# Projection groups of a segmented memory transformer regrouped: five groups instead of seven, one left unit per segment, and a new order of all items

## The chip, the cores and the metric

The kernel runs on one core of one Trainium2 chip. The time is device microseconds of one execution on that core; the time of a version is the median of its runs. The profile is of one execution.

The engines are named as the profile names them: PE is TensorE (matmuls), PEld its weight loads, DVE VectorE, ACT ScalarE, POOL GpSimd, SP the engine that issues nearly all DMAs here.

## The reference, cut to what matters

The model is 640 wide. Branch A is attention over 64 segments of 32 rows. Every segment puts 8 memory rows in front of its 32 rows, computes Q, K and V for 32 heads of 192, masks, takes the softmax, multiplies by V and projects back with Wo. The first 8 rows of the result are the memory of the next segment, so the segments are a serial chain. Branch B is a gated feed-forward network, and a gate mixes the two.

```
for s in range(n_seg):
    h = concat([mem, x[:, 32*s : 32*s + 32]])
    q, k, v = h @ Wq, h @ Wk, h @ Wv            # 32 heads x 192 = 6144 columns each
    p = softmax(where(mask, q @ k.T * scale, -1e9))
    o = (p @ v) @ Wo
    mem = o[:, :8]
    outs.append(o[:, 8:])
a = concat(outs)
b = (gelu(x @ w_gate) * (x @ w_up)) @ w_down
return g * a + (1 - g) * b                      # g = sigmoid(x . gate_w)
```

## The kernel before, in words

**Start.** The feed-forward branch is computed first and its rows are stored in DRAM. While it runs, weights of the attention are loaded. Then the loop over the 64 segments begins.

**What is "left".** Of a segment's 32 rows of x, the last 8 (the left rows) don't fit beside the 24 others and the 8 memory rows in the 32 rows that one projection handles. Their Q and K don't depend on the memory. They are computed ahead, for four segments at once (a group g of four segments has 4 x 8 = 32 left rows), in left units: one unit is Q and K of one eighth-group of heads, and needs five items `lf` (k = 0..4, two lists of four matmuls each, L899 and the helper L226), then two items `le` that evict and transpose the rows (ACT L904, DVE L906) and store them in DRAM (L910, or L1300 for two halves in mid-segment). Where units are placed is said by LUNIT: for every place (the segment number modulo 4) a map from unit number to head group. Their V (`Vl`) is computed beside V in segments of place 0; one head group's is computed at the end of place 3 (items `vb`, L1034). The output projection of the left rows is done in place 3 beside the ordinary one (`wo_left`).

**Head groups and pieces.** The 32 heads are four groups of 8. For each group, Q, K and V come from five weight pieces (k = 0..4, 128 rows x 1536 columns, 384 KB); the Wo matrix is 16 pieces of 480 KB. Not all fit: the pieces of the first and the last head group share places in SBUF (13 of their 15 projection pieces, and 3 Wo pieces). When the matmul that reads a piece is issued, `swap_loads` (through `load_piece`, L611) puts a load of the partner into SP's queue; odd segments run through the head groups backwards, so every segment loads 16 pieces. For the first group's K the issue is held back until the group's last item, so that Q pieces go first.

**Projection items.** An item ("g", n, k) runs k-step k of projection group n. GROUPS[n] lists which (matrix, head group) pairs it holds: matrix 0 is Q, 1 is K, 2 is V. All lists of a step use the same 32 rows as weights, so the first list loads them (L1061) and the others keep them (`_matmul_kept`, L226). Each list is four matmuls of 384 columns in four column strips of TensorE. After the last step, ACT evicts each result from PSUM, V first where the group has it (L1084 for V, L1081 for Q and K).

**The other items**, in the order of one head group's way: `tq` and `tk` transpose Q and K rows (DVE L1095; POOL L1098 copies part of Q); `sc` puts the mask and the scores in PSUM (L1106, L1114, L234, L1121), and DVE takes maximum and difference (L1133, L1135); `ex` is the rest of the softmax (ACT L1145, DVE L1147, L1149, L1151, L1152); `pt` transposes the probabilities on TensorE (L1168, L1173) and ACT evicts them (L1186); `pv` is the value product (L1201, L1203, evicted by ACT L1212 and, for the last group, also DVE L1217); `wo` is the output projection (L1230 for the first three groups in two items each, L1253 for the last). After the last `wo`, DVE adds (L1395) and transposes (L1399) the new memory into the operand of the next segment.

**What sets the order.** PROG is a list written out by hand, one for all segments; every engine gets its instructions in the order of this list and waits on semaphores. Items of other places are skipped. PSUM banks are handed out by `misc_bank`: the least recently used of banks 0 to 3, bank 4 in places 1 and 2 (in place 3 for groups below 3), bank 7 for groups 0 and 1, leaving out those held by an open left unit. An `le` item behind the last of the other items in PROG is put off until after the segment's end.

## Time and profile before

| | |
|---|---|
| median of 3 runs | 1770.06 us (1767.09 to 1770.34) |
| profiled execution | 1771.21 us |
| its span, first to last instruction | 1769.4 us |
| granted TensorE clock, mean over the span | 0.997 |
| first projection matmul of segment 0 | 178.3 us into the span |
| last matmul of segment 63 | 1763.0 us into the span |
| mean length of a segment in place 0, 1, 2, 3 (segments 4 to 59) | 25.12, 24.94, 23.38, 25.64 us |
| bytes moved by DMA | 499.58 MB, mean 282 GB/s |

The span is what the profile's times refer to; the time of an execution is a little longer. A segment's length is from its first projection matmul to that of the next one.

In the profile a group is a source line with an engine, an operation and a shape; for each it gives busy time, mean length of one instruction, and the idle time of the engine before it with what ended that idle time. Where no semaphore ended it, the profile writes "issue". The lengths of matmuls are modelled and overlap, so the pace of TensorE is read from the starts of successive matmuls.

### The profile page before, as it was taken

The numbers are of one execution on the slowest core, as the hardware profiler recorded it, in microseconds if no ns is written. First come the engines' busy times: TensorE is split into PE (matmuls) and PEld (weight loads), VectorE is DVE, ScalarE is ACT, GpSimd is POOL, SyncE is SP. The second block draws the span as 40 slices with busy tenths as digits, with TensorE's granted clock in tenths as the row PEclk, the third lists the DMA queues.
The fourth block names the chain that finished last, engine by engine and source line by source line (L and its number), as shares of the span: only waits on it lengthen the run. The fifth ranks groups of instructions, "written<-read, shape, count | busy, mean of one in ns | idle before, by whom it ended". The sixth has DMA issues, their size and how long they took to land.

```text
span 1769.4 us, 80660 instructions
## 1 busy us (share of the span) xinstructions
PE 1606.2 (91%) x39162; PEld 798.4 (45%) x31501; DVE 959.9 (54%) x2934; ACT 803.3 (45%) x1835; POOL 400.6 (23%) x1358
## 2 busy tenths in 40 slices
PE   9999899989998999889999998988998899989987
PEld 4554444444444444444444444444444444444443
DVE  2222655556565655556555555555565655655554
ACT  3222544545444544445444544444444454444443
POOL 1100222222222222222222222222222222222222
PEclk9999999999999999999999999999999999999999
DMA  9914987888778887878778886878787887879776
GB/s 319 310 45 153 328 314 258 318 306 292 275 271 310 298 312 254 308 289 313 279 273 293 306 314 226 318 283 300 275 284 288 296 315 259 312 276 326 283 277 236
DMA packets 271313, 499.58 MB, mean 282 GB/s; under 512 B 105304, under 2 KB 132208, under 8 KB 270960
## 3 DMA queue, kind: packets, MB, share of 16 engines
q1 hardware_dynamic: 267832, 491.34, 78.2%
q8 instruction: 276, 4.52, 1.0%
q10 hardware_dynamic: 3128, 3.09, 0.5%
q14 instruction: 77, 0.63, 0.1%
HBM read 473.22 MB, written 21.11 MB: 279 GB/s over the span
## 4 chain that ended last, share of the span: by engine, by line
PE 66%; DVE 17%; issue 6%; DMA 5%; ACT 4%; POOL 1%; DVEq 0%; SPq 0%; ACTq 0%; POOLq 0%
PE ps L1061 18%; PE ps L226 14%; PE ps L1230 8%; DMA arena<-in_A_Wo_dram 4%; PE ps L818 3%; PE ps L1201 3%; PE ps L815 3%; PE ps L899 3%; DVE ps L1135 2%; PE ps L1106 2%; DVE arena L1133 2%; PE ps L833 2%; DVE arena L1147 2%; PE ps L1253 2%; DVE arena L1095 2%
## 5 line engine op out<-in xcount | busy, mean ns | idle before, releaser
L1061 PE MATMUL ps<-arena 128*32 128x384 bf16 x9940 | 727.7, 328 | 52.2 <-DVE arena L1399 33.6
L226 PE MATMUL ps<-arena 128*32 128x384 bf16 x7680 | 595.3, 327 | 7.8 <-DVE arena L1239 3.5
L1061 PEld LDWEIGHTS ps<-arena 128*32 128x32 bf16 x9940 | 259.5, 97 | 377.0 <-issue 238.3
L1095 DVE STREAM_TRANSPOSE arena<-arena 128x384 bf16<-128x384 bf16 x512 | 270.6, 557 | 151.3 <-ACT arena L1081 150.3
L1081 ACT ACTIVATE arena<-ps 128x384 bf16<-128x384 f32 x512 | 236.2, 489 | 213.6 <-PE ps L1061 193.2
L1230 PE MATMUL ps<-arena 128*32 128x320 bf16 x6144 | 294.7, 300 | 15.1 <-issue 12.4
L1145 ACT ACTIVATE ps<-ps 104x160 f32<-104x160 f32 x256 | 71.9, 281 | 285.3 <-DVE ps L1135 285.3
L1230 PEld LDWEIGHTS ps<-arena 128*32 128x32 bf16 x6144 | 163.3, 96 | 76.8 <-issue 19.2
L1133 DVE TENSOR_REDUCE arena<-ps 104x4 f32<-104x160 f32 x256 | 82.9, 324 | 163.0 <-PE ps L1121 163.0
L1212 ACT ACTIVATE arena<-ps 128x480 bf16<-128x480 f32 (+1 forms) x256 | 137.0, 535 | 42.5 <-PE ps L1203 37.8
L1098 POOL COPY arena<-arena 64x160 bf16<-64x160 bf16 x256 | 81.3, 318 | 325.3 <-DVE arena L1095 314.2
L1186 ACT ACTIVATE arena<-ps 128x448 bf16<-128x448 f32 x192 | 104.2, 543 | 99.7 <-PE ps L1173 99.1
L1220 POOL COPY arena<-arena 128x96 bf16<-128x96 bf16 x256 | 68.2, 266 | 356.8 <-ACT arena L1212 267.6
L1084 ACT ACTIVATE arena<-ps 128x384 bf16<-128x384 f32 x256 | 125.1, 489 | 26.4 <-PE ps L1061 21.1
L1147 DVE TENSOR_REDUCE arena<-ps 104x4 f32<-104x160 f32 x256 | 83.0, 324 | 93.4 <-ACT ps L1145 93.4
L1201 PE MATMUL ps<-arena 128*64 128x160 bf16 x1536 | 122.1, 242 | 12.1 <-ACT arena L1186 5.8
L1201 PEld LDWEIGHTS ps<-arena 128*64 128x64 bf16 x1536 | 80.8, 109 | 89.1 <-issue 31.6
L899 PE MATMUL ps<-arena 128*32 128x384 bf16 x1280 | 112.7, 332 | 2.4 <-issue 2.4
L956 POOL COPY arena<-arena 128x96 bf16<-128x96 bf16 x256 | 70.3, 275 | 194.1 <-PE ps L1121 130.2
L1203 PE MATMUL ps<-arena 128*64 128x64 bf16 x1536 | 104.8, 194 | 3.9 <-issue 3.9
L1239 DVE TENSOR_TENSOR arena<-ps,arena 64x160 f32<-64x160 f32 x160 | 50.8, 317 | 75.2 <-ACT arena L1236 60.9
L906 DVE STREAM_TRANSPOSE arena<-arena 128x384 bf16<-128x384 bf16 x128 | 73.7, 576 | 31.7 <-ACT arena L904 27.5
(88 smaller groups left out, 2040.7 us busy)
## 6 DMA issues: line engine op xcount, KB each, us to landing
arena<-in_A_Wk_dram SPq DMA_DIRECT2D x335, 384.0 KB, 7.3
arena<-in_A_Wv_dram SPq DMA_DIRECT2D x335, 384.0 KB, 9.1
arena<-in_A_Wo_dram SPq DMA_DIRECT2D x205, 480.0 KB, 6.4
arena<-in_A_Wq_dram SPq DMA_DIRECT2D x209, 384.0 KB, 5.1
arena<-left_qk_scratch SPq DMA_DIRECT2D x126, 96.0 KB, 3.0
left_qk_scratch<-arena SPq DMA_DIRECT2D x49, 192.0 KB, 2.4
left_qk_scratch<-arena SPq DMA_DIRECT2D x30, 96.0 KB, 5.9
ffn_b_scratch<-arena ACTq DMA_DIRECT2D x16, 160.0 KB, 3.8
```

What stands on the lines that cost most here:

```text
L226: return e.add_instruction(mybir.InstMatmult(name=nm, start_tensor_calc=like["start"], stop_tensor_calc=stop, tile_size=(128, 32), tile_po ...
L899: fns.append(lambda e, outp=outp, rhs=rhs, j=j: e.matmul(outp, lhs, rhs, start=(k == 0), stop=(k == KT - 1), tile_position=(0, 32 * j)))
L1061: fns.append(lambda e, outp=outp, rhs=rhs, j=j: e.matmul(outp, lhs, rhs, start=(k == 0), stop=(k == KT - 1), tile_position=(0, 32 * j)))
L1081: S_.add("act", lambda e, m=m, bk=bk: e.activation(out=rows_sb[m], in_=ps[:, bk, 0:384], func=ACTF.Copy), reads=[r_ps[bk]], writes=[r_rows ...
L1084: S_.add("act", lambda e, i=i, bk=bk: e.activation(out=v_sb[i % NVB].rearrange("p (c n) -> p c n", c=3), in_=ps[:, bk, 0:384].rearrange("p ...
L1095: S_.add("dve", lambda e: e.transpose(out=dst[:, :, 0:L], in_=rows_sb[m].rearrange("p (c r) -> p c r", r=L)), reads=[r_rows[m]], writes=[r ...
L1133: S_.add("dve", lambda e: e.tensor_reduce(out=mxs, in_=S3, axis=AX.X, op=ALU.max), reads=[rb], writes=[rst], name="smax max")
L1147: S_.add("dve", lambda e: e.tensor_reduce(out=sms, in_=S3, axis=AX.X, op=ALU.add), reads=[rb], writes=[rst], name="smax sum")
L1201: return [lambda e: e.matmul(full, v[:, e0:e0 + 64], PTm[:, i], start=True, stop=False, tile_position=(0, 64 * i), skip_group_check=True), ...
L1203: lambda e: e.matmul(part, vl[:, e0:e0 + 64], PTl[:, i], start=False, stop=True, tile_position=(0, 64 * i), skip_group_check=True)]
L1212: S_.add("act", lambda e: e.activation(out=apx(u[:, 0, 0, :], [[R, na], [3 * R, 4], [1, R]]), in_=ps[:, A, 0:na * W].rearrange("p (c t r) ...
L1230: fns.append(lambda e, i=i, t=t, j=j, gv=gv: e.matmul(ps[32 * j:32 * j + 32, bank, 0:2 * DJ].rearrange("p (h n) -> p h n", h=2), lhs2[i], ...
```

## The change

Three things change, all of them data of the schedule; no instruction gets another shape.

1. GROUPS goes from seven groups to five. Q and K of a head group always stand in one group, with the V of the head group before: (Q0, K0), (V0, Q1, K1), (V1, Q2, K2), (V2, Q3, K3), (V3). Before, K2 and K3 were groups of their own and Q2 and Q3 stood with the preceding V.
2. LUNIT has one left unit in every place: head groups 3, 0, 2, 1 in places 0, 1, 2, 3. Before, place 1 had two (1 and 0) and place 3 none. The units that place 3 owes are computed ahead of the loop for the first groups, so five units stand there instead of four.
3. PROG is written anew. The scores of head group 1 stand just ahead of value product 0, the scores of 2 and the P transpose of 1 stand inside the fourth projection group, and value product 1 follows that group. The last Wo item is the last of all items, so every `le` item stands ahead of the segment's end, and none is in mid-segment.

```diff
-    GROUPS = [[(0, 0), (1, 0)], [(2, 0), (0, 1), (1, 1)], [(2, 1), (0, 2)], [(1, 2)], [(2, 2), (0, 3)], [(1, 3)], [(2, 3)]]
+    GROUPS = [[(0, 0), (1, 0)], [(2, 0), (0, 1), (1, 1)], [(2, 1), (0, 2), (1, 2)], [(2, 2), (0, 3), (1, 3)], [(2, 3)]]
...
-    PROG = [("g", 0, 0), ("g", 0, 1), ("g", 0, 2), ("g", 0, 3), ("g", 0, 4), ("tq", 0), ("g", 1, 0), ("tk", 0),
-            ("g", 1, 1), ("g", 1, 2), ("sc", 0), ("g", 1, 3), ("ex", 0), ("g", 1, 4), ("tq", 1), ("g", 2, 0),
-            ("g", 2, 1), ("g", 2, 2), ("lf", 1, 0, 0), ("pt", 0), ("g", 2, 3), ("tk", 1), ("g", 2, 4), ("g", 3, 0),
-            ("sc", 1), ("g", 3, 1), ("lf", 1, 0, 1), ("g", 3, 2), ("ex", 1), ("g", 3, 3), ("g", 3, 4), ("g", 4, 0),
-            ("lf", 1, 0, 2), ("pv", 0), ("lf", 1, 0, 3), ("g", 4, 1), ("tk", 2), ("g", 4, 2), ("pt", 1), ("g", 4, 3),
-            ("tq", 2), ("g", 4, 4), ("sc", 2), ("ex", 2), ("lf", 1, 0, 4), ("pv", 1), ("g", 5, 0), ("le", 1, 0, 0),
-            ("g", 5, 1), ("lf", 0, 1, 0), ("g", 5, 2), ("wo", 0, 0), ("le", 1, 0, 1), ("tq", 3), ("pt", 2), ("g", 5, 3),
-            ("wo", 0, 1), ("g", 5, 4), ("pv", 2), ("tk", 3), ("lf", 0, 1, 1), ("lf", 1, 1, 0), ("wo", 1, 0), ("sc", 3),
-            ("lf", 2, 1, 0), ("wo", 1, 1), ("g", 6, 0), ("lf", 2, 1, 1), ("lf", 1, 1, 1), ("g", 6, 1), ("ex", 3),
-            ("g", 6, 2), ("wo", 2, 0), ("lf", 1, 1, 2), ("pt", 3), ("g", 6, 3), ("lf", 2, 1, 2), ("g", 6, 4),
-            ("wo", 2, 1), ("lf", 2, 1, 3), ("lf", 1, 1, 3), ("pv", 3), ("lf", 0, 1, 2), ("lf", 2, 1, 4), ("lf", 1, 1, 4),
-            ("vb", 0), ("le", 1, 1, 0), ("vb", 1), ("vb", 2), ("vb", 3), ("le", 1, 1, 1), ("le", 2, 1, 0),
-            ("lf", 0, 1, 3), ("lf", 0, 1, 4), ("wo", 3, 0), ("le", 2, 1, 1), ("le", 0, 1, 0), ("wo", 3, 1), ("le", 0, 1, 1),
-            ("vb", 4)]
+    PROG = [("g", 0, 0), ("g", 0, 1), ("g", 0, 2), ("g", 0, 3), ("g", 0, 4), ("g", 1, 0), ("g", 1, 1), ("g", 1, 2),
+            ("tq", 0), ("tk", 0), ("sc", 0), ("g", 1, 3), ("ex", 0), ("g", 1, 4), ("tq", 1), ("g", 2, 0),
+            ("g", 2, 1), ("tk", 1), ("g", 2, 2), ("pt", 0), ("g", 2, 3), ("g", 2, 4), ("sc", 1), ("tq", 2),
+            ("pv", 0), ("g", 3, 0), ("tk", 2), ("g", 3, 1), ("g", 3, 2), ("ex", 1), ("lf", 2, 1, 0), ("sc", 2),
+            ("pt", 1), ("g", 3, 3), ("ex", 2), ("g", 3, 4), ("pv", 1), ("lf", 2, 1, 1), ("lf", 1, 1, 0), ("tk", 3),
+            ("lf", 0, 1, 0), ("tq", 3), ("lf", 2, 1, 2), ("wo", 0, 0), ("lf", 1, 1, 1), ("pt", 2), ("lf", 3, 1, 0),
+            ("wo", 0, 1), ("g", 4, 0), ("pv", 2), ("sc", 3), ("wo", 1, 0), ("wo", 1, 1), ("wo", 2, 0), ("ex", 3),
+            ("g", 4, 1), ("wo", 2, 1), ("lf", 0, 1, 1), ("g", 4, 2), ("pt", 3), ("g", 4, 3), ("g", 4, 4),
+            ("lf", 1, 1, 2), ("lf", 2, 1, 3), ("lf", 3, 1, 1), ("lf", 0, 1, 2), ("lf", 3, 1, 2), ("lf", 3, 1, 3),
+            ("vb", 0), ("lf", 2, 1, 4), ("pv", 3), ("lf", 1, 1, 3), ("lf", 0, 1, 3), ("le", 2, 1, 0),
+            ("lf", 1, 1, 4), ("le", 1, 1, 0), ("vb", 1), ("le", 1, 1, 1), ("vb", 2), ("le", 2, 1, 1),
+            ("lf", 0, 1, 4), ("vb", 3), ("lf", 3, 1, 4), ("vb", 4), ("wo", 3, 0), ("le", 3, 1, 0), ("le", 0, 1, 0),
+            ("le", 0, 1, 1), ("le", 3, 1, 1), ("wo", 3, 1)]
...
-    LUNIT = ({1: 3}, {0: 1, 1: 0}, {1: 2}, {})
+    LUNIT = ({1: 3}, {1: 0}, {1: 2}, {1: 1})
```

## The prediction, as it was put on record

> **What bounds the kernel.** I read the page, then the busy time of four successive segments, then the timelines of all engines inside one of them, then the DMA rows, the waits and the clock. A list below is four matmuls of 384 columns (one weight piece against the 32 rows of a segment); P0 to P3 is the segment number modulo 4; times inside a segment count from its first projection matmul.

> ```profile
> PE 1606.2 (91%) x39162; PEld 798.4 (45%) x31501; DVE 959.9 (54%) x2934; ACT 803.3 (45%) x1835; POOL 400.6 (23%) x1358
> ...
> PE 66%; DVE 17%; issue 6%; DMA 5%; ACT 4%; POOL 1%; DVEq 0%; SPq 0%; ACTq 0%; POOLq 0%
> ```
> TensorE is the bound on average, with a third of the chain elsewhere. The same by segment, P0 to P3 in order:
> ```profile
> 969.70:994.85 25.15, 22.87 (x612) 11.82 (x492) 15.49 (x49) 12.26 (x29) 5.75 (x20) 1.00 0.79 279
> 994.85:1020.74 25.89, 22.51 (x592) 10.89 (x452) 15.21 (x47) 12.47 (x29) 5.05 (x19) 1.00 0.81 284
> 1020.74:1043.60 22.86, 20.93 (x553) 10.00 (x434) 13.79 (x44) 11.55 (x27) 6.43 (x21) 1.00 0.89 318
> 1043.60:1067.88 24.28, 23.00 (x629) 12.54 (x530) 12.54 (x42) 11.03 (x26) 6.67 (x22) 1.00 0.81 296
> ```
> The first column after the window is the length, the next the matmul busy time. Over segments 4 to 59 the mean lengths are 25.12, 24.94, 23.38 and 25.64 us, together 99.08; 64 segments are 1585 of the 1769.4 us.

> Two other things bound a segment. **Weights**: 13 projection pieces and 3 output pieces come in per segment, each into the place of one just used.
> ```profile
> L611 SPq DMA_DIRECT2D arena<-in_A_Wk_dram x5: 333/432/442, 1021.3 to 1025.8; - x5
> ...
> DMA to landing us min/median/max: 4.3/5.7/6.7
> ```
> ```profile
> L611 SPq DMA_DIRECT2D arena<-in_A_Wo_dram x3: 328/430/432, 1034.5 to 1035.3; - x3
> ...
> DMA to landing us min/median/max: 5.1/6.0/6.7
> ```
> The last K piece is issued at 1025.8 and lands 6.7 later, 11.75 us into this P2 segment; the last Wo piece lands at 1042.0, 21.3 in. The pieces queue behind each other (about 1 us each), so their landing hangs on when the first group frees places, not on when they are wanted. Medians over all segments: last K piece at 12.48, 13.83, 12.82, 12.43 (P0 to P3; earliest of P3 11.54), last Wo piece at 21.9, 23.6, 21.7, 21.5.

> **Refill of TensorE's instructions**:
> ```profile
> PEld ps L1061 <- issue: 238.3, 819, 2.6
> ...
> PEld ps L1168 <- DVE arena L1152: 82.1, 148, 1.0
> ```
> ```profile
> 1008.96 0.66 PE L1061 MATMUL ps<-arena 128*32 128x384 bf16 x9 [1.04 <-issue]
> ```
> Numbering all matmuls and weight loads, every stop of this kind falls on the same instruction of 256 (the instruction queue's packets are 16 KB). There are 267 such borders in the loop; 87 cost over 0.25 us, 73 us in all: 0.82, 0.90, 0.68, 2.16 us per segment in P0 to P3. The stop depends on how fast the 256 before it went: over 6 us it is 0.02 on average, 5 to 5.5 us 0.41, 4 to 4.5 us 1.00.

> **Part by part. Weight loads.** Before, 5 of a segment's 12 projection lists per k keep the weights of the list before; after, 7 (groups of 2, 3, 3, 3, 1). That removes 2x5x4 = 40 loads per segment, 2560 in all. I take no gain:
> ```profile
> 1020.92 0.34 PE L226 MATMUL ps<-arena 128*32 128x384 bf16 x4
> 1021.08 0.34 PE L1061 MATMUL ps<-arena 128*32 128x384 bf16 x4
> ...
> 1021.24 0.34 PE L226 MATMUL ps<-arena 128*32 128x384 bf16 x4
> ...
> 1021.40 0.34 PE L1061 MATMUL ps<-arena 128*32 128x384 bf16 x4
> ```
> Lists with own weights (L1061) and kept ones (L226) both start 0.163 us after the one before. The other end is 2560 x 26 ns (259.5 us over 9940 loads) = 67 us gained. [...]

> **Work per segment.** From the timelines: 60 lists x 0.163 = 9.78; four scores at 0.48, four P transposes at 0.10, four value products at 0.52; six Wo items at 0.407; the last two with their entry 0.96; from the last matmul to the next segment's first 0.87 (DVE's sums and transposes). That is 18.45. A left unit is 5 x 0.325 = 1.63; P0 adds 15 left-value lists, 2.45; P3 adds 7 left Wo items at 0.407 and 5 lists, 3.67. Before: 22.5, 21.7, 20.1, 22.1; lengths less work leave stalls of 2.6, 3.25, 3.3, 3.5. After, P1 loses a unit to P3: 22.5, 20.1, 20.1, 23.75. The sum is the same; the start-up gains a unit and the loop loses one.

> **K3 moved forward.** After, Q3 and K3 stand in the fourth group. Ahead of its end are 55 lists (8.95), three scores (1.44), two P transposes (0.2) and one value product (0.52): 11.1 us, 11.4 in P2 with a left item. Its last K list can't start before the last K piece lands, 12.4 to 12.8, and ends 0.16 later. The same pieces were wanted at 14 to 15.6 before, and TensorE's weight loads waited 1.9 us for them in the whole trace. Behind the waiting list stand, on TensorE, all that follows in the segment, and through it the evictions of V2, Q3 and K3 on ACT and everything that these release. P1's 13.83 becomes about 12.7, because the store that delayed its first K load to 1.62 (0.54 elsewhere) is no longer issued behind the segment's end. So TensorE waits 1.7, 1.55, 1.5 us in P1, P2, P3; none to 0.1 in P0, whose left-value lists (10 x 0.163) and bank wait bring it to about 13. This wait covers softmax 1: from score 1's end DVE needs 0.34 + 0.34, two transposes 1.05, then 0.34 + 0.19 + 0.29 + 0.18 = 2.7, over the 2.45 of TensorE work laid beside it.

> **What goes.** The wait for P transposes 2 and 3 (0.9, 0.55, 0.8, 0.4 by place): softmax 2 ends near 13.95, its transpose is wanted at 14.5 to 15, and softmax 3 (2.1 us) has three or four Wo items beside it. P1's lateness of Wo pieces goes too: two mid-segment stores leave SP's queue and the first K piece starts 1.1 earlier, so the last Wo lands near 21.7. With the 1.3 from the last Wo item to the next segment this is a floor of about 23.0.

> **What is late next.** P0 keeps its wait for the bank of the left sums before Q2 (released by DVE L1239, 0.4) and for the copied Q of score 0 (POOL L1098, 0.17; in the others it is in the rest). P0: the left rows are all ahead of the Z sums on DVE now; two transposes (0.49 apart) end 1.6 after the first last-Wo item starts, the sums were due at 1.13: 0.5. Value product 3 waits for V3's eviction (0.49): 0.3 in P0, 0.45 in P1, 0.15 in P2. P2: the bank of value product 1 is V2's, evicted only after the group's last V list: 0.35; nothing stands between value product 3 and the last Wo: 0.55 for its eviction; small ones 0.5 (P transpose 2's eviction 0.15, softmax 3 0.2, Z 0.15). P1: 0.35 of the same small ones, 0.1 for Wo. Moved DMAs: the left stores go out just before the next segment's stage load on SP; P0's first K piece then lands like P2's, 4.7 instead of 4.1, which its work covers.

> **Refill.** 40 instructions fewer of 1072 per segment. Behind the K wait P3 has 640 in 11.3 us (4.5 us per 256), P1 about 480 in 9.4 (5.0): as dense as before. I take 0.85, 0.6, 0.7, 2.1. Ends: half of it, or half more.

> **Sum.** Stalls after: P0 refill 0.85, bank 0.4, Qz 0.17, V3 0.3, tail 0.5, rest 0.25 = 2.45; P1 0.6 + 1.7 + 0.45 + 0.35 + 0.1 + 0.25 = 3.45; P2 0.7 + 1.55 + 0.35 + 0.55 + 0.15 + 0.5 = 3.8; P3 2.1 + 1.5 + 0.3 = 3.9. Lengths: 24.95, 23.55, 23.9, 27.65 = 100.05 against 99.08: +0.97 per four, 16 times +15.5. The profiled execution took 1771.2 (span 1769.4), 1.1 over the median of 1770.06; so 1770.06 + 15 is **1785**, its own range 1767 to 1802.

> **Rivals.**
> A, refill stops halve (0.13): -36, **1749**. For: fewer instructions, and the K wait stretches the blocks that hold it. It decides at 6 us per block of 256, in the half behind the K wait. Against: that half is as dense as before.
> B, on the other side as well (0.11): the K pieces come in time. If the last one lands by 11.0, P3 gets 1.5 back, P2 0.4, P1 0.1: 32 us, **1753**. Against: the earliest of P3 was 11.54.
> C, slower (0.18): the refill stops grow by half, or the clock gate drops in the waits: **1822**.
> ```profile
> 1685.80:1689.20 3.40, 1.79 (x64) 1.22 (x60) 1.67 (x7) 0.97 (x3) 1.14 (x3) 1.00 0.11 28
> 1689.20:1692.60 3.40, 3.32 (x44) 0.91 (x24) 0.71 (x4) 0.14 (x1) 0.72 (x3) 0.50 0.49 135
> ```
> A 3.4 us window with 1.79 busy is followed by one with a granted clock of 0.50; this happens three times in the loop, 1.7 us lost each. One in two of P1 to P3's waits would cost 24 x 1.7 = 41. Against: a K wait of 3.8 us holds 2.5 us of work. [...]
> D, weight loads set the pace after all (0.03): -67, **1718**.

> **Chances.** Forecast 0.55, of it 0.09 within and 0.02 below the 0.2% (3.5 us) that a measurement of this kernel can tell from no change. Faster 0.13 + 0.11 + 0.03 + 0.02 = 0.29, same 0.09, slower 0.44 + 0.18 = 0.62. The range takes in A, B and most of C: 1748 to 1820.

> **What would show it.** Weight loads 28,941 and equal pace of L1061 and L226; waits of L226 or L1061 for in_A_Wk of some 1.5 us in P1 to P3, near zero in P0; no wait left at L1168 for L1152 in the second half; P1 shorter by 1.4, P3 longer by 2. I am wrong if K waits stay under 0.5, if P3 grows by less than 1, or if refill stops leave 50 to 95 us.

## The result, and the profile after

The changed kernel takes 1777.74 us (median of 8 runs, 1774.39 to 1786.39); the kernel before took 1770.44 us beside it (8 runs). The ratio is 1.0046, 95% interval 1.0024 to 1.0068: slower, by 7 us, where 15 were forecast. The profiled execution took 1774.39 us (span 1772.6), the shortest of the eight, so the two traces (1771.21 and 1774.39) show only 3 us of the 7; where the other 4 lie, no trace shows.

Lines of the changed kernel are one lower than those of before from L611 on (L1061 is L1060, L1399 is L1398); helper L226 keeps its number. The page of the changed kernel, the busy line and the two lines of the chain, by engine and by source line:
```profile
PE 1580.3 (89%) x39181; PEld 741.7 (42%) x28941; DVE 945.5 (53%) x2934; ACT 781.4 (44%) x1835; POOL 399.5 (23%) x1358
...
PE 59%; DMA 24%; DVE 8%; ACT 5%; issue 3%; SPq 1%; POOL 0%; DVEq 0%; ACTq 0%; POOLq 0%
DMA arena<-in_A_Wk_dram 20%; PE ps L226 14%; PE ps L1060 12%; PE ps L1229 11%; PE ps L1200 4%; DVE arena L905 3%; PE ps L898 3%; PE ps L814 3%; PE ps L817 3%; DMA arena<-in_A_Wo_dram 3%; PE ps L832 2%; PE ps L1105 2%; ACT arena L1185 1%; DVE arena L1238 1%; ACT arena L903 1%
```
2560 weight loads are gone, as counted. DMA's share of the chain went from 5% to 24%: in 45 of the 64 segments the chain now runs through the landing of a K piece; before, it did in one. The same by segment (28 to 31, P0 to P3; columns as in the prediction):
```profile
875.58:899.14 23.56, 22.11 (x613) 10.65 (x454) 15.75 (x50) 11.94 (x28) 5.74 (x20) 1.00 0.88 306
899.14:922.35 23.21, 20.20 (x553) 8.94 (x393) 13.43 (x44) 11.28 (x27) 5.74 (x20) 1.00 0.86 311
922.35:946.59 24.24, 20.55 (x552) 8.97 (x392) 13.54 (x44) 11.02 (x27) 5.74 (x20) 1.00 0.85 299
946.59:973.39 26.80, 24.14 (x669) 12.13 (x509) 13.45 (x44) 11.55 (x28) 6.61 (x22) 1.00 0.75 266
```
P1 and P2 hold 3.0 and 3.7 us without a matmul. Where they went shows in the waits of TensorE's matmuls (total us, times, longest):
```profile
PE ps L226 <- DMA arena<-in_A_Wk_dram: 51.9, 101, 1.8
PE ps L1060 <- DVE arena L1398: 48.0, 63, 1.3
...
PE ps L1105 <- POOL arena L1097: 3.9, 1, 3.9
```
and in those of its weight loads:
```profile
PEld ps L1060 <- issue: 349.4, 922, 2.2
...
PEld ps L1167 <- DVE arena L1151: 21.0, 56, 0.4
```
The first row is the new wait for K. It counts only gaps in which no modelled matmul runs; taken from the starts of the matmuls, as the forecast was, the wait is larger: 0.19, 1.71, 1.35 and 1.62 us per segment in P0 to P3. L1105's single wait belongs to the very first score. The wait of the P transposes for softmax (82.1 us, up to 1.0) is down to 21.0 us, never above 0.4. The "issue" row of the weight loads grew from 238.3 to 349.4 us, yet the refill stops fell: a weight load that waits only because TensorE's queue ahead of it waits (for K, say) is put down to "issue" too. In segment 31 the loads of 956.37 and 958.31, behind K waits of 0.47 and 1.04 us, stand there with 1.02 and 1.84. So that row is no measure of the refill, and was none before (238.3 us, where the stops came to 73); the stops have to be counted at the borders of 256 instructions, as in the prediction. TensorE's semaphore instructions in the trace (25 before, 40 after) count in that numbering too: with them the stops of the loop stay at one number of 256 from its start to its end, in both traces.

The K wait itself, in the timeline of TensorE in segment 31 (P3), which begins at 946.59:
```profile
954.90 0.35 PE L1060 MATMUL ps<-arena 128*32 128x384 bf16 x4
955.07 0.50 PE L226 MATMUL ps<-arena 128*32 128x384 bf16 x8
...
956.36 0.33 PE L226 MATMUL ps<-arena 128*32 128x384 bf16 x4 [0.47 <-DMA arena<-in_A_Wk_dram]
956.52 0.33 PE L1060 MATMUL ps<-arena 128*32 128x384 bf16 x4
956.68 0.33 PE L226 MATMUL ps<-arena 128*32 128x384 bf16 x4
958.05 0.33 PE L226 MATMUL ps<-arena 128*32 128x384 bf16 x4 [1.04 <-DMA arena<-in_A_Wk_dram]
```
The K3 list of k-step 1 waits, V2 and Q3 of step 2 follow, and the K3 list of step 2 waits again, until 11.5 us into the segment. The DMA rows of segment 30 (P2), K pieces and then, from a second answer, Wo pieces:
```profile
L610 SPq DMA_DIRECT2D arena<-in_A_Wk_dram x5: 432/432/832, 922.9 to 926.3; - x5
...
DMA to landing us min/median/max: 3.2/8.1/9.1
```
```profile
L610 SPq DMA_DIRECT2D arena<-in_A_Wo_dram x3: 327/430/432, 937.7 to 938.6; - x3
...
DMA to landing us min/median/max: 3.7/4.8/6.4
```
All K pieces are asked for in the first 4 us of the segment and the median takes 8.1 us to land: they stand behind one another.

From the traces, in us (means of segments 4 to 59, "first" and "last" being segments 0 to 3 and 60 to 63 together):

| | P0 | P1 | P2 | P3 | four | first | last | refill stops in all |
|---|---|---|---|---|---|---|---|---|
| before | 25.12 | 24.94 | 23.38 | 25.64 | 99.08 | 99.8 | 104.2 | 73.0 |
| predicted | 24.95 | 23.55 | 23.9 | 27.65 | 100.05 | | | about 68 |
| after | 24.77 | 23.79 | 23.85 | 26.32 | 98.73 | 106.2 | 105.7 | 46.5 |

So the steady segments became faster, 1387.1 to 1382.2 us over 56 of them, and the first four slower by 6.4, the last four by 1.5. Of the 6.4, segment 0 has 3.5 and segment 3 has 4.75 (28.51 instead of 23.76: the unit, the K wait and one refill stop of 2.3); segments 1 and 2 gave 1.9 back.

**The start.** Segment 0 took 31.1 us instead of 27.6. SP's queue at the start, before and then after:
```profile
171.30 2.25 SPq L611 DMA_DIRECT2D arena<-in_A_Wo_dram  x5
174.71 5.24 SPq L910 DMA_DIRECT2D left_qk_scratch<-arena  x4
```
```profile
170.51 2.25 SPq L610 DMA_DIRECT2D arena<-in_A_Wo_dram  x5
173.84 9.52 SPq L909 DMA_DIRECT2D left_qk_scratch<-arena  x5
```
Then DVE's timeline of the changed kernel:
```profile
181.78 1.19 DVE L905 STREAM_TRANSPOSE arena<-arena 128x384 bf16<-128x384 bf16 x2 [3.04 <-DMA left_qk_scratch<-arena]
...
185.37 1.04 DVE L1094 STREAM_TRANSPOSE arena<-arena 128x384 bf16<-128x384 bf16 x2
```
and TensorE's:
```profile
186.39 0.32 PE L1105 MATMUL ps<-arena 128*40 128x160 bf16 x1 [3.92 <-POOL arena L1097]
```
Five left units stand ahead of the loop now, and there are four staging places. The transposition of the fifth waits on DVE for the store of the first, which was issued at 173.8 behind five Wo loads and landed 7.9 us later. Behind it on DVE stand the columns of the gate (2.4 us, there before too) and the transposition of Q and K of segment 0, and behind that score 0, which waits 4.17 us from start to start. From 184.5 on the granted clock is 0.50 for 6.8 us.

### The profile page after: what moved, and what is told of

It reads as the page before. It is cut to its first block, busy times and chain, and to the rows that moved or that the text cites. A ratio compares the mean times of both kernels' runs of the same rounds, so it can differ in the third digit from the quotient of the medians.

```text
span 1772.6 us, 78041 instructions
## 1 busy us (share of the span) xinstructions
PE 1580.3 (89%) x39181; PEld 741.7 (42%) x28941; DVE 945.5 (53%) x2934; ACT 781.4 (44%) x1835; POOL 399.5 (23%) x1358
## 4 chain that ended last, share of the span: by engine, by line
PE 59%; DMA 24%; DVE 8%; ACT 5%; issue 3%; SPq 1%; POOL 0%; DVEq 0%; ACTq 0%; POOLq 0%
DMA arena<-in_A_Wk_dram 20%; PE ps L226 14%; PE ps L1060 12%; PE ps L1229 11%; PE ps L1200 4%; DVE arena L905 3%; PE ps L898 3%; PE ps L814 3%; PE ps L817 3%; DMA arena<-in_A_Wo_dram 3%; PE ps L832 2%; PE ps L1105 2%; ACT arena L1185 1%; DVE arena L1238 1%; ACT arena L903 1%
## 5 line engine op out<-in xcount | busy, mean ns | idle before, releaser
L226 PE MATMUL ps<-arena 128*32 128x384 bf16 x10240 | 734.8, 328 | 70.2 <-DMA arena<-in_A_Wk_dram 51.9
L1060 PE MATMUL ps<-arena 128*32 128x384 bf16 x7380 | 584.6, 330 | 57.1 <-DVE arena L1398 48.0
L1060 PEld LDWEIGHTS ps<-arena 128*32 128x32 bf16 x7380 | 200.3, 97 | 459.0 <-issue 349.4
L1094 DVE STREAM_TRANSPOSE arena<-arena 128x384 bf16<-128x384 bf16 x512 | 264.2, 554 | 122.9 <-ACT arena L1080 120.2
L1080 ACT ACTIVATE arena<-ps 128x384 bf16<-128x384 f32 x512 | 223.8, 492 | 215.2 <-PE ps L1060 203.4
L1229 PE MATMUL ps<-arena 128*32 128x320 bf16 x6144 | 264.7, 300 | 11.9 <-issue 11.8
L1229 PEld LDWEIGHTS ps<-arena 128*32 128x32 bf16 x6144 | 156.0, 97 | 64.9 <-issue 21.6
L1083 ACT ACTIVATE arena<-ps 128x384 bf16<-128x384 f32 x256 | 124.8, 487 | 23.5 <-PE ps L1060 16.5
L905 DVE STREAM_TRANSPOSE arena<-arena 128x384 bf16<-128x384 bf16 x128 | 74.0, 578 | 50.8 <-ACT arena L903 44.5
L1252 PE MATMUL ps<-arena 128*32 128x160 bf16 x3072 | 77.6, 237 | 21.0 <-ACT arena L1211 10.1
```

Of the source, the lines that this page charges most:

```text
L226: return e.add_instruction(mybir.InstMatmult(name=nm, start_tensor_calc=like["start"], stop_tensor_calc=stop, tile_size=(128, 32), tile_po ...
L905: S_.add("dve", lambda e: e.transpose(out=dst.rearrange("p q c i -> p c q i"), in_=rowl.rearrange("p (c r) -> p c r", r=L)), reads=[r_rowl ...
L1060: fns.append(lambda e, outp=outp, rhs=rhs, j=j: e.matmul(outp, lhs, rhs, start=(k == 0), stop=(k == KT - 1), tile_position=(0, 32 * j)))
L1080: S_.add("act", lambda e, m=m, bk=bk: e.activation(out=rows_sb[m], in_=ps[:, bk, 0:384], func=ACTF.Copy), reads=[r_ps[bk]], writes=[r_rows ...
L1083: S_.add("act", lambda e, i=i, bk=bk: e.activation(out=v_sb[i % NVB].rearrange("p (c n) -> p c n", c=3), in_=ps[:, bk, 0:384].rearrange("p ...
L1094: S_.add("dve", lambda e: e.transpose(out=dst[:, :, 0:L], in_=rows_sb[m].rearrange("p (c r) -> p c r", r=L)), reads=[r_rows[m]], writes=[r ...
```

## The experiments

The kernel before ran beside each of these at 1764 to 1766 us; ratios are against it. The profiled execution of a run is one of its runs, so a sum of four lengths can be 0.6 us off what its median would give (the runs without V loads, and with the Wo loads behind all units, were profiled in their slowest execution).

### Where the weight loads of the loop are left out

The K pieces are not loaded in the loop (the products use what lies in their places, so the result is not the reference's); the second kernel does the same for V.
```diff
+            if other[0] == 1:
+                loaded[slot_id[other]] = other
+                continue
```
(`== 2` in the second.) Expected without the K loads:

> The changed kernel with the five K pieces per segment no longer loaded (head groups 0 and 3 use whatever K weights lie there, so the result is not the reference's; five of sixteen loads a segment are left out). Theory: the wait of the K lists in group 3 is on the path. The trace shows it at 0.19, 1.71, 1.35, 1.62 us in P0 to P3; it goes, the wait of P transpose 1 for softmax 1 (0.5 to 0.7) is uncovered: P0 24.5, P1 22.3, P2 22.7, P3 25.0, time 1700 to 1715. Rival 1: the wait is covered by something later (last Wo pieces, which still land near 17 here instead of 22, would not hold it, so: softmax 1 and the evictions): lengths fall by under 0.5 each, time above 1755. Rival 2: it is the load traffic as such that slows the segment; then leaving out the V pieces does the same.

Expected without the V loads:

> The changed kernel with the five V pieces per segment no longer loaded (result not the reference's; the same 1.9 MB per segment less as in the run without K loads). Theory: K lists wait as before (1.3 to 1.7 us in P1 to P3), the last Wo pieces land 5 us earlier, so only the Wo waits (0.07, 0.38) and part of the refill stops go: time 1760 to 1773. Rival 2 (traffic as such): the same time as without the K loads, 1700 to 1715.

| | time | ratio | P0 to P3 | K waits P0 to P3 | refill stops |
|---|---|---|---|---|---|
| after | 1777.74 | 1.0046 [1.0024, 1.0068] | 24.77, 23.79, 23.85, 26.32 | 0.19, 1.71, 1.35, 1.62 | 46.5 |
| no K loads | 1676.39 | 0.9515 [0.9452, 0.9579] | 23.62, 22.05, 22.17, 24.31 | none | 10.6 |
| no V loads | 1728.22 | 0.9810 [0.9729, 0.9891] | 24.00, 23.50, 23.24, 25.88 | 0.28, 1.54, 1.17, 1.40 | 13.9 |

Two executions stand behind each of the two times, 11 and 18 us apart. Both came out below their expectations, in the main for one reason: with a quarter less traffic the stops for refill fall from 46.5 us to 11 and 14. A thousand us in the middle of the loop, after and then without V loads (window; length, busy time and count of PE, PEld, DVE, ACT, POOL; granted clock, DMA share, GB/s):
```profile
400.00:1400.00 1000.00, 888.10 (x24060) 414.51 (x17620) 567.45 (x1798) 461.76 (x1108) 241.49 (x828) 0.99 0.82 290
```
```profile
400.00:1400.00 1000.00, 906.07 (x24674) 418.52 (x18010) 582.34 (x1846) 475.04 (x1139) 248.31 (x850) 0.99 0.65 217
```
At a DMA share of 0.82 the borders whose 256 instructions took 5 to 5.5 us stop for 0.31 us on average, and 0.41 at 4.5 to 5; at 0.65 the same blocks stop for 0.15 and 0.17. So the same block stopped for less here when less else was moved; that fits a refill which queues with the other loads, but where it queues isn't shown. Without V loads the K waits hardly move, so they are not made by the V loads behind them. Without K loads, whose refill stops are as rare, the four segments are another 4.47 us shorter in the traces (96.62 less 92.15), where the K waits of the run without V sum to 4.39. By the medians the difference is 52 us, 3.2 per four. So the K wait is on the path, some three quarters of it or more; the scatter of two executions carries no closer price. Rival 2 is nearly half right: by the ratios 94 us go without K loads, and 42 without V loads. The page of the kernel without K loads shows what remains:
```profile
PE 74%; DVE 12%; ACT 7%; DMA 4%; issue 3%; POOL 0%; ACTq 0%; DVEq 0%; SPq 0%; POOLq 0%
```

### The units alone

The kernel before with its groups and order, and the left units placed as after: P1's unit 0 taken out, one in P3 beside P2's.
```diff
-    LUNIT = ({1: 3}, {0: 1, 1: 0}, {1: 2}, {})
+    LUNIT = ({1: 3}, {1: 0}, {1: 2}, {1: 1})
...
```
(The dots stand for its `lf` and `le` items in PROG, which are moved to match.)

> The kernel before with only the left units redistributed: one in every place as in the change, the unit of P3 beside that of P2 in the old order; groups and order are the old ones. Theory: P1 24.9 to 23.5 (a unit of 1.63 less, no stores in mid-segment, first K load at 0.55), P3 25.6 to 27.2 (a unit more and no wait to fill), and the start-up loses about 4 us as in the change (a fifth unit in a staging place whose store has not landed): time 1775 to 1782. Rival 3: the units balance at no cost and all of the loss is in groups and order: P3 grows by less than 1, time 1752 to 1765.

1778.13 us, 1.0095 [1.0058, 1.0131]. P1 fell by 0.95 (24.94 to 23.99), P3 rose by 1.05 (25.64 to 26.69), the four took 99.26, and the first four segments 104.3: segment 0 again 31.1. P1 gave back less than the unit's 1.63 because one thing that I had put down to the unit stayed: its first K load is still asked for 1.62 us into the segment, since the last `le` item of P0 still stands behind the segment's end in this order. The units alone thus cost nearly 1%. Groups and order may give about half of it back (1.0095 to 1.0046), but the intervals overlap a little (1.0058 to 1.0068), and the two ratios come from different sessions. The two traces place only 3 us of the 14: the first four segments 4.5 more, the 56 behind them 2.5 more, the last four 3.7 less. The profiled execution is the shortest of this kernel (1774.54), and the trace of before is of a longer one (1771.21) than the median beside this run (1764.04); where the other 11 us lie stays open.

### The start

Two kernels move the five early Wo loads. The first asks for them behind all left units:
```diff
     gate_loads()
-    load_residents(2)
...
+    load_residents(2)
     gate_cols()
```

> The changed kernel with the loads of the residents of class 2 (five Wo pieces) issued behind the left units ahead of the loop, not ahead of them. Theory: the left store of the first unit no longer queues behind these 2.4 MB, so the transposition of the fifth unit, which reuses its staging place, doesn't wait 3.0 us and score 0 of segment 0 not 4.2 us: segment 0 falls from 31.1 to 27 or 28, time 3 to 5 below the changed kernel's 1777.7; the segments from 4 on stay (24.8, 23.8, 23.85, 26.3). Rival 4: the store waits for its own packets, segment 0 stays at 31.

1779.55 us, 1.0098 [1.0066, 1.0129]. The stores now land in 2.1 to 2.8 us and score 0 waits 1.68 us instead of 4.17, as the mechanism says. But the Wo loads come 10 us later, and segment 0 waits for V pieces (3.45 us) and for Wo (4.8): 36.8 us, in the slowest of its seven executions. The second kernel asks for them right behind the first store:
```diff
         left_store(g, o, b)
         if n == 0:
+            load_residents(2)
```

> The changed kernel, with the class 2 output weights asked for right behind the first left unit's store instead of before all left units. Theory (score 0 of the first segment waits for a store of left values that lands 7.9 us after its issue because it stands behind five output loads in the DMA queues; the loads need be behind the one store only): that store lands in about 2 to 3 us, score 0 waits under 2 us instead of 4.17, the output loads come at most 3 us later than in the changed kernel, the first segment takes 27 to 29 instead of 31.1; 2 to 4 us below the changed kernel, 1.002 to 1.003 of the kernel before. Rival: the loads come late again and what score 0 gives back is lost at the output items, as in the run that put them behind all units; first segment 31 or more.

1772.86 us, 1.0052 [1.0029, 1.0076]: no different from the changed kernel. The first store lands in 2.3 us and score 0 waits 1.52, but the later stores now land behind the Wo loads (7.8 to 9.4 us after their issue), and the Q and K lists of segment 0 wait 3.4 us for DVE and ACT instead; segment 0 takes 30.9. So what the trace showed as one wait is a shortage of queue time: in each of the three orders that I tried another transfer is late. The expected gain was not there.

### The weight loads

The changed kernel, in which only the second list of a group keeps weights:
```diff
-            S_.add("pe", mms(m, bk, htile(k), k, g_, n > 0),
+            S_.add("pe", mms(m, bk, htile(k), k, g_, n == 1),
```

> The changed kernel with weights kept only for the second list of a group instead of all but the first: 4 lists x 5 k per segment load their own weights again, 1280 loads more in 64 segments (28941 to some 30200), same order, same data. Theory (a list has one pace of 0.163 us with or without own weights; what more instructions do is bring more borders of 256): pace unchanged, segment lengths within 0.3 of the changed kernel's, refill 46 to 60 us, time 0 to 15 us above the changed kernel's (1.004 to 1.013 of the kernel before). Rival D of the prediction (loads at 26 ns each count): 1280 x 26 ns = 33 us, half of the 67 of the prediction, 1.023 of the kernel before. Rival: the K wait swallows what stands ahead of it, and nothing changes at all.

The count in this expectation is wrong: 3 lists of four loads per k-step go back, 3 x 4 x 5 x 64 = 3840 loads; 1280 is the distance to the kernel before. At 26 ns each, rival D's price would be 100 us. The page:
```profile
L1060 PE MATMUL ps<-arena 128*32 128x384 bf16 x11220 | 780.3, 330 | 111.0 <-DMA arena<-in_A_Wk_dram 45.8
L226 PE MATMUL ps<-arena 128*32 128x384 bf16 x6400 | 558.1, 330 | 13.5 <-DVE arena L1181 7.8
L1060 PEld LDWEIGHTS ps<-arena 128*32 128x32 bf16 x11220 | 293.1, 97 | 501.4 <-issue 175.4
```
1797.54 us, 1.0181 [1.0150, 1.0211]: 24 us more than the changed kernel by the ratios. P0 to P3 are 25.54, 23.88, 24.15, 27.35 (four: 100.91), and the refill stops rose from 46.5 to 72.9 us, by place 1.64, 0.67, 0.59, 1.66 against 1.04, 0.63, 0.31, 0.93. The K waits are a little shorter (0.26, 1.52, 1.29, 1.27; together 4.34 instead of 4.87). The 26.4 us of refill are of the size of the whole cost, and no price of the loads themselves shows: both kinds of list still start 0.163 us apart. One such stop, in the timeline of TensorE in segment 28:
```profile
925.59 0.32 PE L1060 MATMUL ps<-arena 128*32 128x384 bf16 x1 [2.40 <-issue]
```
So rival D was wrong in its mechanism and the theory was wrong in its size: a weight load more costs 6 to 7 ns here (24 and 26.4 us over 3840), nearly all of it through the refill. What the 2560 loads that the change removes are worth is then about 2560/3840 of 24, an estimate of 16 us.

### Work put into the K wait

The first two Wo items don't need K3. Here they stand ahead of its last k-steps:
```diff
-            ("pv", 0), ("g", 3, 0), ("tk", 2), ("g", 3, 1), ("g", 3, 2), ("ex", 1), ("lf", 2, 1, 0), ("sc", 2),
-            ("pt", 1), ("g", 3, 3), ("ex", 2), ("g", 3, 4), ("pv", 1), ...
+            ("pv", 0), ("g", 3, 0), ("tk", 2), ("g", 3, 1), ("wo", 0, 0), ("g", 3, 2), ("ex", 1), ("lf", 2, 1, 0), ("sc", 2),
+            ("pt", 1), ("wo", 0, 1), ("g", 3, 3), ("ex", 2), ("g", 3, 4), ("pv", 1), ...
```

> The changed kernel with the first two output items alone moved into the K wait (before the K3 lists are done) in all places; everything else as in the changed kernel. Theory (K wait is idle TensorE time, 1.7, 1.35, 1.6 in P1 to P3; the two items are 0.81 us of work): P3 26.32 less 0.8 to 1.2, P1 and P2 less 0 to 0.6 since their last output piece lands at 22 and 1.3 us follow; P0 same; sum 98.73 to about 97.0, 25 us; 1750 to 1757, 0.989 to 0.993 of the kernel before. Rival (the items only hand on their lateness, since what ends the segment is the softmax chain and value product 3): sum within 0.4 of the changed kernel.

1761.00 us, 0.9988 [0.9973, 1.0003]. This is faster than the changed kernel (the intervals don't touch: 0.6%, 10 us), and no different from the kernel before. P0 to P3: 25.19, 23.04, 23.40, 26.20; P1 and P2 gave about what was expected (0.75 and 0.45), P3 a tenth of it, and P0 lost 0.42. Its granted clock is higher than that of the changed kernel (0.993 to 0.997 against 0.988 to 0.993), so part of the 10 us may be the clock. The waits of TensorE's matmuls:
```profile
PE ps L1200 <- ACT arena L1185: 32.1, 63, 1.1
PE ps L226 <- DMA arena<-in_A_Wk_dram: 16.5, 33, 1.1
```
The K wait fell from 51.9 to 16.5 us, and value product 2 now waits 32.1 us for the eviction of P transpose 2. ACT's timeline in segment 31 (937.52 to 963.50) shows why:
```profile
951.19 0.49 ACT L1083 ACTIVATE arena<-ps 128x384 bf16<-128x384 f32 x1 [0.67 <-PE ps L1060]
951.58 0.87 ACT L1080 ACTIVATE arena<-ps 128x384 bf16<-128x384 f32 x2
952.32 0.59 ACT L1211 ACTIVATE arena<-ps 128x480 bf16<-128x480 f32 x1
952.77 0.57 ACT L1185 ACTIVATE arena<-ps 128x448 bf16<-128x448 f32 x1
```
V2, Q3, K3 and value product 1 are evicted in a row, released by the last K3 list, and the P transpose stands behind them. With the Wo items gone from this place TensorE has nothing to do beside it. The lateness of K was handed on along ACT.

### More work ahead of score 3

Two kernels move left items as well. The first puts three of the five left items of P1 and P2 and one Wo item into the K wait, a fourth left item behind P transpose 2, one Wo item between the last K3 step and value product 1, exchanges the units of P1 and P3, and asks for the early Wo loads behind the first store (that edit is the one shown above):
```diff
-            ... ("g", 3, 1), ("g", 3, 2), ("ex", 1), ("lf", 2, 1, 0), ("sc", 2), ("pt", 1), ("g", 3, 3), ("ex", 2), ("g", 3, 4), ("pv", 1), ...
+            ... ("g", 3, 1), ("lf", 1, 1, 0), ("lf", 2, 1, 0), ("wo", 0, 0), ("g", 3, 2), ("lf", 1, 1, 1), ("lf", 2, 1, 1), ("ex", 1), ("sc", 2), ("pt", 1), ("lf", 1, 1, 2), ("lf", 2, 1, 2), ("g", 3, 3), ("ex", 2), ("g", 3, 4), ("wo", 0, 1), ("pv", 1), ...
-    LUNIT = ({1: 3}, {1: 0}, {1: 2}, {1: 1})
+    LUNIT = ({1: 3}, {1: 1}, {1: 2}, {1: 0})
```

> The changed kernel, with the work beside the K wait of P1 and P2 and the waits of the second half changed: P3's left unit of the start is of another head group than P1's (P1 keeps none as in the changed kernel, but the places' head groups 0 and 1 are exchanged), four left items of P1 and P2 stand in the K wait instead of behind value product 3, the first output item stands in the K wait in all places and the second between the last projection list and value product 1, and the class 2 output weights are asked for after the first left unit's store. Theory (the K wait is a wait for a landing at a fixed time, so TensorE work that does not need K costs nothing there, and value product 1's bank and value product 3's eviction are the next waits): P0 24.5, P1 and P2 about 23.4 (last output piece at 22 plus 1.3), P3 25.0 (1.3 less than 26.32), first segment 27 to 28 instead of 31.1; 1745 to 1755, 0.986 to 0.991 of the kernel before. Rival 1, refill: denser blocks behind the wait bring the stops back to 73 us, 1.7 per four segments more, and the time is 1765 to 1775. Rival 2, weights: the output pieces land later because something else frees them, and the segments stay at the changed kernel's lengths.

1776.74 us, 1.0072 [1.0052, 1.0092]; P0 to P3 are 25.24, 23.84, 23.80, 26.45. The expectation's "P1 keeps none" is wrong: every place has one unit, as in the changed kernel. The gain did not come. Rival 1 is out, since the refill stops are 47.3 us; rival 2 has the lengths right but not the cause, since the last Wo piece lands at 21.4 to 21.7. The K waits fell to 0.1 to 0.5. In P1 and P2 the second half, from which the left items went, now has waits: 1.0 and 0.77 us at the last V3 list (a P transpose is evicted from its bank by DVE L1181), 0.82 at value product 3 for V3's eviction, 0.65 at value product 2. The second keeps the order of the run with the two Wo items in the K wait, without the edits of the last one, and moves two left items of P0 and of P3 into the hole ahead of value product 2:
```diff
-            ... ("pt", 2), ("lf", 3, 1, 0),
+            ... ("pt", 2), ("lf", 3, 1, 0), ("lf", 0, 1, 1), ("lf", 0, 1, 2), ("lf", 3, 1, 1), ("lf", 3, 1, 2),
```

> The run with the first two output items in the K wait, and in P0 and P3 two left items more (two lists each, 0.33 us) moved from behind the output items to the place between P transpose 2 and value product 2, where that run had waits of 0.60 and 0.83 us for the eviction of P transpose 2 on ACT (it stands there behind the evictions of V2, Q3, K3 and value product 1). Theory (score 3 can't start before about 16 us, since K3 lands at 12.6 to 12.9 and is evicted, transposed and copied first; what stands ahead of score 3 is free up to there, and what stands behind it is paid): P3 26.20 to 25.5, P0 25.19 to 24.7, P1 and P2 unchanged at 23.0 and 23.4; sum 97.82 to 96.6, 20 us; about 1740 to 1748, 0.988 to 0.992 of the kernel before. Rival (the end of these segments hangs on softmax 3, V3's eviction and the next sums, not on TensorE's work behind score 3): the waits move behind the output items, sum within 0.4 of 97.82, 0.998.

1775.07 us, 1.0042 [1.0021, 1.0063]. The rival won, and more: P0 rose to 25.89 and P3 to 26.47. The hole closed (0.60 to 0.06 in P0, 0.83 to 0.44 in P3), and in its place stand, in P0, 0.55 us at the last V3 list for DVE L1181 and 0.53 at value product 3 for DVE L1027 (left values), in P3 0.39 at the left values for V3's eviction. Work that was moved out of the end of a segment no longer covers softmax 3 and V3's eviction there. No version that I ran and that computes the reference beats the kernel before clear of noise.

## Why the prediction held, and where it was wrong

The time lies in the forecast range and is slower, as forecast, and the K wait came as it was priced. The place of the loss is another matter, and there the sign was luck: the forecast has it in the loop, where four segments were to take 0.97 us more, and in the traces they take 0.35 less. What the traces show of the loss is at the ends, for which the forecast had no term of its own. Two of its three signs of being wrong came as well: P3 grew by 0.68, under the 1 that it named, and the refill stops came to 46.5 us, under its 50 to 95. Two errors of opposite sign meet: the refill was taken too large, and the start too cheap.

**Weight loads.** The count was right to the instruction, and so was the equal pace. "I take no gain" was wrong: the gain, some 16 us by the run with own loads, comes through the refill and not through the loads' own time. The 67 us of rival D are not there: lists with own weights and with kept ones still start 0.163 us apart.

**Work per segment.** P1 and P3 exchanged a unit as reckoned; P1 became 1.15 shorter where 1.39 was forecast, P3 0.68 longer instead of 2.0.

**K3 moved forward.** Waits of 0 to 0.1, 1.7, 1.55, 1.5 were forecast and 0.19, 1.71, 1.35, 1.62 came. P1's first K load goes out at 0.58 instead of 1.62 and its last lands at 12.67 (12.7 forecast). The runs without K and without V loads show that some three quarters of the wait or more are paid.

**What goes.** Confirmed: the matmuls of P transposes 2 and 3 wait 0.1 us at most for softmax where it was 0.4 to 0.9, and P1's last Wo wait fell from 0.36 to 0.07.

**What is late next.** Right were the bank of the left sums in P0 (0.43 for 0.4), the bank of value product 1 in P2 (0.36 for 0.35) and value product 3's eviction in P2 (0.62 for 0.55). V3's eviction was smaller (0.19, 0.09, 0.05 for 0.3, 0.45, 0.15). Not foreseen: 0.57 at the left item of P1 behind the last V3 list, which waits for a P transpose's eviction by DVE L1181; 0.31 in P1 to P3 at the first K2 list, released by V0's eviction (L1083); 0.38 in P2 for the last Wo piece. They make up for what was smaller, by chance: P1 and P2 came within 0.24 and 0.05 of the forecast.

**Refill: the step that failed.** Taken were 0.85, 0.6, 0.7, 2.1; measured 1.04, 0.63, 0.31, 0.93. P3's 1.17 is nearly the whole of its 1.33 below the forecast, and over 14 such segments 16 of the 18.5 us between +0.97 and -0.35 per four. I judged it by instructions per us in the half behind the K wait, found "as dense as before", and let the 40 missing instructions count for nothing. By the run with own loads, which keeps the K waits and has P3 at 1.66, the 2560 loads account for 2560/3840 of 26.4, some 18 of the 26.5 us of the fall (an estimate, taken as linear). Rival A's effect thus came to nearly three quarters: it wanted 36, and 26.5 came. Its other half, that the K wait stretches the blocks which hold it, wasn't tried alone. Between 12.5 and 16 us into a segment, where a block holds the wait, the stops sum to about 13 us before and 3.5 after, which fits; but with own loads and the wait kept they are about 11 again, so most of that fall goes with the loads.

**Start: the term that was too small.** I wrote "the start-up gains a unit and the loop loses one", and took it as equal. The unit's 1.63 us of work is; its staging place is not. Segment 0 costs 3.5 us more, and it comes with the fifth unit: the run with the units alone shows the same segment 0 (31.1). That it is the store behind the Wo loads, and the slow clock behind that wait, is argued from the trace: neither version that shortened the wait brought segment 0 below 30.9.

**Rival C.** Up to segment 63, the granted clock in the loop is 0.50 for ten stretches of 3.41 us after and for three before; at up to 1.7 us (half of 3.41) for each of the seven more, that is at most 12 us. Two of the ten follow a K wait, where the rival had one in two of 42, so a fall follows a wait far more rarely than the rival had it. The lower clock itself is a rival that stays open: all eight executions of the changed kernel have a mean granted clock of 0.988 to 0.993, those of the kernel before beside the experiments 0.994 to 0.999. In the run with the Wo loads behind the first store the time goes with it, from 1761 us at 0.994 to 1784 us at 0.988. No run changes the clock alone, so how much of the 7 us is the clock stays open. The clock isn't needed for such a loss: the run with the units alone is as slow at 0.995 to 0.998. **Rival B** is out: the last K piece lands at 12.5 to 12.7. **Rival D** is out by the run with own loads.

Put together for the profiled executions: forecast +15.5; the 56 steady segments came 18.5 lower, the ends 6 higher; seen +3.2. The medians differ by 7.3.

## What to carry to other kernels

A matmul that is moved ahead of the landing of its weights waits for the landing, and here the wait could be priced ahead from issue and landing times (1.7, 1.55 and 1.5 us forecast, 1.71, 1.35 and 1.62 seen). Filling it was worth little here, since evictions and softmax behind the late list set the rest of the segment (the K wait fell from 51.9 to 16.5 us, and 32.1 us of waiting for P transpose 2's eviction came): ask which chain ends last before moving work, because work taken from the end can uncover what it covered there. And a total with the right sign is no proof of its terms: see in which segments the loss lies. The 3840 weight loads more left the pace of the lists at 0.163 us and still went with 26.4 us more of refill stops, so an instruction's time in its pipe is not all to count. And of a unit of work that is moved to the start, count its buffers and its place in the DMA queue, not only its matmuls: a unit of 1.63 us of work went with 3.5 us more in segment 0 here.

## What the runs showed of the hardware

**Refill went with the traffic.** The stops at every 256th instruction sum to 46.5 us at 290 GB/s and to 13.9 at 217 GB/s with the same program on TensorE, and 3840 more weight loads bring 26.4 us. The row of the instruction queue on the page (packets, MB, share) moves with the number of instructions; before, after, and with own loads:
```profile
q8 instruction: 276, 4.52, 1.0%
```
```profile
q8 instruction: 266, 4.36, 1.0%
```
```profile
q8 instruction: 281, 4.60, 1.0%
```
The 2560 loads less are 10 packets less, the 3840 more are 15 packets more: 256 instructions each, of 16 KB. That the stops wait for these packets is read from their times: at the borders where the next instruction of TensorE started over 0.5 us after the one before (70 in the loop before, 43 after), it started 1.2 to 2.0 us after the end of a packet; at those where it started within 0.3 us, a median of 2.5 and 3.1 us and up to 10.9 after one.

**A store behind loads.** A store of 192 KB landed 2.1 to 2.8 us after its issue where the Wo loads came behind all units, and 7.9 us behind five loads of 480 KB in the changed kernel.
